# Local attention and an ELU feed-forward layer: the values of two neighbouring tiles in one visit, the global keys' values as 32-row products

## The chip, the cores and the metric

The kernel runs on one core of one Trainium2 chip. A core has five engines that run their own instruction streams: PE (TensorE, matrix products), DVE (VectorE), ACT (ScalarE), POOL (GpSimd) and SP (SyncE, which here issues the transfers). The metric is the device time of one execution in microseconds. Before the change it is 972.03 us, the median of three runs (970.75 to 972.27).

## The reference

Eight batches, eight heads of 64 dimensions, 512 local and 32 global positions, all float32. A global query looks at all 544 keys. A local query looks at the 32 global keys and at the local keys no more than 32 positions away. The attention's output is the input of two dense layers with an ELU between them.

```python
s_g = scale * q_g @ concat(k_g, k_l).T ;  out_g = softmax(s_g) @ concat(v_g, v_l)
s_ll = where(|i - j| <= 32, scale * q_l @ k_l.T, -1e9)
s_l = concat(scale * q_l @ k_g.T, s_ll) ;  out_l = softmax(s_l) @ concat(v_g, v_l)
x = concat(out_g, out_l) as (4608 tokens, 512)
h = x @ w_in                          # 512 -> 2048
g = where(h > 0, h, exp(min(h, 0)) - 1)
out = g @ w_out                       # 2048 -> 512
```

## The kernel before

**Two streams, woven together.** `attention()` and `ffn_stream()` are Python generators that emit instructions. The loop at L867 takes one step of attention, then as many steps of the feed-forward stream (FFN) as a table `PACE` asks for by then: none in the first 66 steps (the lead, flag `lead`), 180 by step 112, 850 by step 320. Small follow-up work (normalizing, reductions, splits into two float16 parts, conversion of the weights) is put off with `defer(n, fn)`: it is emitted n ticks later, and there is a tick at each FFN step, or at each attention step where no FFN step is due. A planner then orders each engine's queue by this order and its own estimate of when operands are ready, so that in the trace instructions can pass each other. Once attention has ended (flag `alone`), the rest of the FFN runs by itself.

**FFN.** A block is 256 tokens; there are 16 blocks of local tokens and one of all global tokens. `ffn1` (L315) multiplies float16 high and low parts of x and w_in, three products in place of one; the result goes through ACT and DVE (L324 to L357) and is split again. `ffn2` multiplies with w_out, either plainly (L390) or with seven half-size products in place of eight (`ffn2_seven`, L432), the latter once all weights are converted. From then on the seven's sums hold four PSUM banks: both `acc`, one of the two `h`, one of the four `pa`.

**Attention.** A tile is 128 local queries of four heads (one batch b, group of heads g, tile t of four). `slots` lists the tiles in order, with a slot "g" ahead for the global queries' scores of a batch and group (`stage_ga`, L641 and L644). In each slot the generator makes four steps, in the order "SVTU":

- **S**, `stage_s`, for the slot's own tile: scores for 64 own and 64 neighbouring keys and 32 global ones (L707), mask, scaling and minimum (L718 on DVE, into the buffer `p`, of which there are three), exponentials (L724 on ACT, deferred by 2 and 3), division by the sum (L731 on POOL and L733 on DVE, deferred by 4).
- **V**, `stage_v`, for the tile three slots back: the values.
- **T**, `stage_t`, for the tile two slots back: four transposes of the probabilities on PE (L747), copied from PSUM to `ptw` (L749). There are two `ptw` buffers.
- **U**, `stage_u`, for the same tile: transposes of the probabilities for global keys (L680) and of the global queries' probabilities (L683, L682), copied to `ptw` and to `ptg` (L684 to L691). `ptg` has one buffer for t = 0 and one for the other t; its last 32 columns, the global queries against global keys, are filled for t = 0 and stay zero in the other buffer.

**The value visit.** For each of the four heads h = 2j + r there are three products, all 128 rows deep and 64 columns wide, on column half r of the array. The first takes the global keys: `v[:, 8 + h, :]` holds the head's 32 global values in rows 32h to 32h + 31 and zeros elsewhere, and 160 columns of `ptg` hold all four heads' probabilities. The other two take the local keys, 96 columns each. All of a tile's products share one bank (`pv`; one of the `h` banks in the lead, a `pa` bank later). ACT copies the local queries' part to `xr` (L779); a tick later DVE adds the global queries' part to `xglob` (L784 for t = 0, L786 after) and takes the tile's absolute maximum (L788). After tile 1 or 3 of the second group a block of x is ready for the FFN; the global block's maximum is taken per two batches (L793).

**Loads.** SP issues every load and nearly every store in program order. `loads(i + 2)` fetches q, k and the global queries two slots ahead; v of a tile (L629, three buffers) is asked for in the tile's own slot, three slots ahead of its use. A transfer that waits for its buffer holds what stands behind it on SP.

Of the kernel before, what the change touches and what calls it, by code (L numbers as in the profile page):

```python
# [14 lines left out]
ALU = mybir.AluOpType  # L15
# [18 lines left out]
LAGT, LAGV = 2, 3  # L34
# [24 lines left out]
def attn_ffn(ctx: ExitStack, tc: tile.TileContext, qT, qgT, kT, vT, w_in, w_out, mask, out):  # L59
# [46 lines left out]
    ptw = [wts.tile([P, 2, 4 * (HQ + 32) + 32], F32, name=f"ptw{i}") for i in range(2)]  # L106
    ptg = [wts.tile([P, PW], F32, name=f"ptg{i}") for i in range(2)]
# [4 lines left out]
    for p in (*ptg, *pkd):  # L112
        nc.gpsimd.memset(p, 0.0)
# [185 lines left out]
    def ffn_stream():  # L299
# [203 lines left out]
        def split_x(blk):  # L503
            xr, mx = ready[blk]
            xh = ffn.tile([P, NC, BLK], F16, name="xh", bufs=NX)
            xl = ffn.tile([P, NC, BLK], F16, name="xl", bufs=NX)
            done = []
            xf, hf, lf = (a.rearrange("p c t -> p (c t)") for a in (xr, xh, xl))

            def s1():  # L510
                all_max(mx[:, 1:2], mx[:, 0:1])

            def s2():
                power(mx[:, 2:3], mx[:, 1:2])
# [7 lines left out]
            nc.vector.tensor_reduce(out=mx[:, 0:1], in_=mx[:, 6:10], op=ALU.max, axis=AX.X)  # L522
# [80 lines left out]
    def new_x():  # L603
        return ffn.tile([P, NC, BLK], F32, name="xr", bufs=3), ffn.tile([P, 10], F32, name="xm", bufs=NX + 4)

    xglob, mglob = wts.tile([P, NC, BLK], F32, name="xglob"), wts.tile([P, 10], F32, name="mglob")

    def attention():
# [17 lines left out]

        def load_v(b, g, t):
            v = apool.tile([P, 12, D], F32, name="v", bufs=3)
            nc.sync.dma_start(v, vT[b, g, t])  # L629
            return v  # L630
# [63 lines left out]
        def stage_s(st, g, t):  # L694
# [17 lines left out]
            pp = apool.tile([P, 4, KW], F32, name="p", bufs=LAGT + 1)  # L712
# [27 lines left out]
        def stage_t(st, g, t):  # L740

            n = tiles[0]
            tiles[0] += 1
            pt, pz = st["pt", g, t] = ptw[n % 2], ptg[t == 0]
            tp = ps_a.tile([P, 512], F32, name="pa")
            for h in range(4):
                nc.tensor.transpose(tp[:, h * P:(h + 1) * P], st["p", g, t][:, h, 0:P], ident)  # L747
# [4 lines left out]
        def stage_v(st, g, t):  # L752

            half = t // 2
            blk = 2 * st["b"] + half
            if (g, t % 2) == (0, 0):
                st["x", half] = new_x()
            xr, mx = st["x", half]
            v = st["v", g, t]
            pt, pz = st["pt", g, t]  # L760
            if lead[0]:
                pv = ps_h.tile([P, 2, BLK], F32, name="h").rearrange("p a b -> p (a b)")
            else:
                pv = ps_a.tile([P, 512], F32, name="pa")
            for j in range(2):
                for i in range(3):
                    for r in range(2):
                        h = 2 * j + r
                        at = j * PW
                        if i == 0:  # L770
                            w, x, o = v[:, 8 + h, :], pz[:, 0:GW], slice(at, at + GW)
                        elif i == 1:
                            w, x, o = v[:, h, :], pt[:, 0, 32 + 96 * h:128 + 96 * h], slice(at, at + 96)
                        else:
                            w, x, o = v[:, 4 + h, :], pt[:, 1, 96 * h:96 + 96 * h], slice(at + HQ, at + GW)
                        nc.tensor.matmul(pv[64 * r:64 * r + 64, o], w, x, start=i == 0, stop=i == 2)  # L776
            pv = pv[:, 0:2 * PW].rearrange("p (j a x) -> p j a x", j=2, a=2)
            xt = xr[:, 2 * g:2 * g + 2, t % 2 * P:(t % 2 + 1) * P]
            nc.scalar.copy(xt.rearrange("p j (a x) -> p j a x", a=2), pv[:, :, :, 0:HQ])  # L779
            xg = xglob[:, 2 * g:2 * g + 2, st["b"] * SG:(st["b"] + 1) * SG]  # L780

            def out():
                if t == 0:
                    nc.vector.tensor_copy(xg, pv[:, :, 0, HQ:])  # L784
                else:
                    nc.vector.tensor_add(xg, xg, pv[:, :, 0, HQ:])  # L786
                i = 6 + 2 * g + t % 2
                nc.vector.tensor_reduce(out=mx[:, i:i + 1], in_=xt, op=ALU.max, axis=AX.XY, apply_absolute_value=True)  # L788
                if g == 1 and t == NT - 1:
                    i = 6 + st["b"] // 2  # L790
                    if st["b"] % 2:
                        c = slice((st["b"] - 1) * SG, (st["b"] + 1) * SG)
                        nc.vector.tensor_reduce(out=mglob[:, i:i + 1], in_=xglob[:, :, c], op=ALU.max, axis=AX.XY,  # L793
                                                apply_absolute_value=True)
                if g == 1 and t % 2 == 1:
                    ready[blk] = xr, mx
                    if blk == NBL - 1:
                        ready[NBL] = xglob, mglob
# [13 lines left out]
        def loads(i):  # L812
# [3 lines left out]
            if s[0] == "g":  # L816
                st["qg", s[2]] = load_qg(s[1], s[2])
                for hp in (2 * s[2], 2 * s[2] + 1):
# [7 lines left out]

        for i in range(AHEAD):
            loads(i)
        for i in range(n + LAGV):
            if i + AHEAD < n:  # L830
                loads(i + AHEAD)
            s0 = slots[i] if i < n else None
            s1 = slots[i - LAGT] if LAGT <= i < n + LAGT else None
            s2 = slots[i - LAGV] if i >= LAGV else None
            for what in "SVTU":
                if what in "TU" and s1 and s1[0] == "l":
                    (stage_t if what == "T" else stage_u)(sts[s1[1]], *s1[2:])
                elif what == "V":
                    if s2 and s2[0] == "l":
                        stage_v(sts[s2[1]], *s2[2:])  # L840
                    if s0 and s0[0] == "l":
                        sts[s0[1]]["v", s0[2], s0[3]] = load_v(*s0[1:])
# [48 lines left out]
def _layout(q_l, k_l, v_l, q_g, k_g, v_g, moe_w_in, moe_w_out):  # L891
# [8 lines left out]
    vG = np.zeros((B, H, NT, 4, 32, D), f)  # L900
# [3 lines left out]
    for t in range(NT):  # L904
        for h in range(H):
            vG[:, h, t, h % 4] = v_g[:, h]
        for half in range(2):
# [3 lines left out]
            for c, key in enumerate([*own, *left, *right] if half == 0 else [*left, *right, *own]):  # L911
                if 0 <= key < SL:
# [7 lines left out]
    vT = np.concatenate([vW.reshape(B, 2, 4, NT, 2, P, D).transpose(0, 1, 3, 5, 4, 2, 6).reshape(B, 2, NT, P, 8, D),  # L920
                         vG.reshape(B, 2, 4, NT, P, D).transpose(0, 1, 3, 4, 2, 5)], axis=4)
    return dict(qT=qT, qgT=qgT, kT=kT, vT=vT, w_in=moe_w_in.view(np.int64), w_out=moe_w_out.view(np.int64), mask=mask)
# [17 lines left out]
```

## Time and profile before

| What | us |
|---|---|
| median of the runs shown (three) | 972.03 |
| the profiled execution | 972.96 |
| its span, first to last instruction | 970.9 |
| PE busy (matrix products) | 927.9, 96% of the span |
| DVE busy | 743.6, 77% |
| ACT busy | 691.7, 71% |
| POOL busy | 264.8, 27% |
| first FFN product (L315) starts at | 80.7 |
| last value product (L776) starts at | 832.9 |

The sum of a change is made against the profiled execution's 972.96 us. Busy times of PE overlap where products run side by side or are pipelined, so what a group of products costs is read from when instructions start, not from the sum of their durations. A row of a group gives the line, engine, operation, written and read tiles, shapes and count, then busy us and mean ns, then idle time just before and who ended it. In the shape of a product, 128*64 says how many rows and columns of the array it takes.

### The profile page before, as it was taken

The numbers are of one execution on the slowest core, as the hardware profiler recorded it, in microseconds if no ns is written. First come the engines' busy times: TensorE is split into PE (matmuls) and PEld (weight loads), VectorE is DVE, ScalarE is ACT, GpSimd is POOL, SyncE is SP. The second block draws the span as 40 slices with busy tenths as digits, with TensorE's granted clock in tenths as the row PEclk, the third lists the DMA queues.
The fourth block names the chain that finished last, engine by engine and source line by source line (L and its number), as shares of the span: only waits on it lengthen the run. The fifth ranks groups of instructions, "written<-read, shape, count | busy, mean of one in ns | idle before, by whom it ended". The sixth has DMA issues, their size and how long they took to land.

```text
span 970.9 us, 23721 instructions
## 1 busy us (share of the span) xinstructions
PE 927.9 (96%) x9216; PEld 742.1 (76%) x9216; DVE 743.6 (77%) x2147; ACT 691.7 (71%) x1666; POOL 264.8 (27%) x484
## 2 busy tenths in 40 slices
PE   5789889899999999999999999999999999999997
PEld 2557465566676788888888888888888888888886
DVE  4987899899957877677777877686777877676665
ACT  4777797776666777677777777677867767666674
POOL 3666193482222311231213122122222211200000
PEclk8889899999999999999999999999999999999999
DMA  6955766531342123111420133113311111000000
GB/s 246 326 189 169 250 235 222 180 122 70 117 146 86 56 94 128 42 32 48 152 98 19 56 108 134 34 41 110 110 57 32 42 34 39 2 22 23 2 23 22
DMA packets 39368, 95.09 MB, mean 98 GB/s; under 512 B 5944, under 2 KB 6456, under 8 KB 39256
## 3 DMA queue, kind: packets, MB, share of 16 engines
q1 hardware_dynamic: 39064, 93.32, 28.5%
q8 instruction: 72, 1.18, 0.5%
q14 instruction: 40, 0.33, 0.1%
q10 hardware_dynamic: 144, 0.13, 0.0%
q0 software_dynamic: 48, 0.13, 0.0%
HBM read 78.36 MB, written 15.20 MB: 96 GB/s over the span
## 4 chain that ended last, share of the span: by engine, by line
PE 72%; DVE 13%; issue 5%; ACT 5%; DMA 3%; POOL 2%; POOLq 0%; SPq 0%; DVEq 0%; ACTq 0%
PE h L315 26%; PE acc L432 13%; PE pa L776 7%; PE h L432 6%; PE acc L390 4%; PE pa L707 4%; PE pa L432 3%; PE pa L315 2%; PE pa L747 2%; DVE gl L336 2%; DMA raw<-w_in 1%; DVE cu L268 1%; PE h L776 1%; POOL p L731 1%; ACT p L724 1%
## 5 line engine op out<-in xcount | busy, mean ns | idle before, releaser
L315 PE MATMUL h<-xh,winh 128*128 128x256 f16 x992 | 270.6, 273 | 1.2 <-ACT hs L325 1.1
L315 PE MATMUL h<-xh,winl 128*128 128x256 f16 x992 | 270.4, 273 | 0.0
L315 PE MATMUL h<-xl,winh 128*128 128x256 f16 x992 | 270.4, 273 | 0.0
L315 PEld LDWEIGHTS <-winh 128*128 128x128 f16 x2176 | 208.1, 98 | 40.2 <-issue 9.5
L731 POOL TENSOR_SCALAR p<-p,sm 128x128 f32<-128x128 f32 x256 | 130.4, 526 | 370.2 <-DVE sm L729 212.7
L333 DVE SCALAR_TENSOR_TENSOR g<-g,hs 128x512 f32<-128x512 f32 x136 | 94.7, 696 | 113.7 <-ACT g L326 113.3
L432 PEld LDWEIGHTS <-gh 128*128 128x128 f16 x1456 | 139.2, 98 | 23.6 <-issue 6.1
L724 ACT ACTIVATE p<-p,m 128x160 f32<-128x160 f32 x256 | 106.5, 419 | 30.8 <-DVE m L718 30.2
L324 ACT ACTIVATE g<-h,xs 128x512 f32<-128x512 f32 x124 | 84.8, 684 | 57.7 <-PE h L315 57.4
L315 PEld LDWEIGHTS <-winl 128*128 128x128 f16 x1088 | 106.5, 98 | 12.9 <-issue 0.5
L336 DVE SCALAR_TENSOR_TENSOR gl<-gs,xs,gh 128x640 f16<-128x640 f32 x104 | 92.4, 888 | 26.8 <-ACT gh L355 26.5
L355 ACT ACTIVATE gh<-gs,xs 128x640 f16<-128x640 f32 x104 | 86.4, 831 | 36.1 <-DVE gs L351 36.0
L354 ACT ACTIVATE gh<-g,xs 128x256 f16<-128x256 f32 x104 | 53.2, 511 | 59.5 <-DVE g L333 57.7
L432 PE MATMUL acc<-wouth,gh 128*128 128x256 f16 (+1 forms) x312 | 88.0, 282 | 0.2 <-ACT gh L355 0.2
L326 ACT ACTIVATE g<-g 128x512 f32<-128x512 f32 x136 | 85.6, 630 | 0.0
L432 PE MATMUL acc<-wouth,gl 128*128 128x256 f16 x312 | 85.1, 273 | 0.2 <-DVE gl L336 0.2
L432 PE MATMUL acc<-woutl,gh 128*128 128x256 f16 x312 | 85.0, 273 | 0.0
L325 ACT ACTIVATE hs<-h,xs 128x512 f32<-128x512 f32 x124 | 84.5, 681 | 0.0
L336 DVE SCALAR_TENSOR_TENSOR gl<-g,xs,gh 128x256 f16<-128x256 f32 (+1 forms) x136 | 76.4, 562 | 7.0 <-ACT gh L340 6.2
L432 PEld LDWEIGHTS <-gl 128*128 128x128 f16 x728 | 71.2, 98 | 12.8 <-DVE gl L336 0.5
L718 DVE CUSTOM_DVE_ANT_0 p<-pa,msk 128x160 f32<-128x160 f32 x228 | 61.4, 318 | 3.3 <-PE pa L707 2.8
L390 PE MATMUL acc<-wouth,gh 128*128 128x512 f16 x128 | 49.8, 389 | 10.8 <-DVE o L398 6.3
(215 smaller groups left out, 2004.2 us busy)
## 6 DMA issues: line engine op xcount, KB each, us to landing
v<-vT SPq DMA_DIRECT2D x64, 384.0 KB, 3.2
k<-kT SPq DMA_DIRECT2D x32, 640.0 KB, 5.1
q<-qT SPq DMA_DIRECT2D x32, 256.0 KB, 5.7
raw<-w_in SPq DMA_DIRECT2D x8, 1024.0 KB, 5.8
raw<-w_out SPq DMA_DIRECT2D x8, 1024.0 KB, 5.7
out<-o SPq DMA_DIRECT2D x32, 256.0 KB, 2.3
od<-o SPq DMA_DIRECT2D x24, 256.0 KB, 2.3
o<-od SPq DMA_DIRECT2D x24, 256.0 KB, 2.7
```

Source lines behind the costliest of these rows:

```text
L315: nc.tensor.matmul(h[:, j, :], wt[:, c, f], xt[:, c, :], start=k == 0, stop=k == 11)
L324: nc.scalar.activation(g, hf, AF.Relu, scale=sc[:, p:p + 1])
L325: nc.scalar.activation(hs, hf, AF.Copy, scale=sc[:, 2 * NP + 1 + p:2 * NP + 2 + p])
L326: nc.scalar.activation(g, g, AF.Exp, scale=-1.0)
L333: nc.vector.scalar_tensor_tensor(out=g, in0=g, scalar=-1.0, in1=hs, op0=ALU.add, op1=ALU.max)
L336: nc.vector.scalar_tensor_tensor(out=dst, in0=src, scalar=sg, in1=hi, op0=ALU.mult, op1=ALU.subtract)
L355: nc.scalar.activation(gh[:, 2:7, :], s, AF.Copy, scale=sg)
L390: nc.tensor.matmul(acc[t], gt[:, s], wt[:, f, :], start=p == first and j == 0 and k == 0, stop=p == last and j == 1 and k == 2)
L432: nc.tensor.matmul(cols, gt, w, start=first, stop=last and k == len(todo) - 1)
L724: nc.scalar.activation(ps[i], ps[i], AF.Exp, bias=m[:, i:i + 1], scale=-1.0, accum_out=s[:, 0, i:i + 1])
L731: nc.gpsimd.tensor_scalar(ps[i][:, 0:P], ps[i][:, 0:P], s[:, 1, i:i + 1], 1.0, ALU.mult, ALU.mult)
L776: nc.tensor.matmul(pv[64 * r:64 * r + 64, o], w, x, start=i == 0, stop=i == 2)
```

## The change

The values of tiles 2*half and 2*half + 1 are computed in one visit, one slot behind the second tile's transposes. In each slot the order is now "TSUV". A pair uses two banks, one for each j (heads 0 and 1, heads 2 and 3), each with both tiles side by side. The global keys' products go first, one per head and tile: 32 rows deep (the head's rows of `ptg`, against the head's rows of a new tile `vg`), 64 columns wide, over 128 columns, or 160 where t = 0. The local keys' products follow as before. `v` loses its four global parts (384 KB to 256 KB a load) and is loaded in the slot of the tile's transposes; `vg` is loaded once per batch and group. ACT still makes two copies a pair, one per bank. DVE sums the global queries' parts of the two tiles with a reduction per bank, and takes one maximum over both tiles; the two halves of a batch are added once per batch. `ptw` and `ptg` get three buffers each, in turn; `ptg` needs no zeros. `p` goes from three buffers to two.

```diff
-LAGT, LAGV = 2, 3
+LAGT = 2
+NPT = 3
-    ptw = [... for i in range(2)]
-    ptg = [... for i in range(2)]
+    ptw = [... for i in range(NPT)]
+    ptg = [... for i in range(NPT)]
-    for p in (*ptg, *pkd):
+    for p in pkd:
         nc.gpsimd.memset(p, 0.0)
...
-            nc.vector.tensor_reduce(out=mx[:, 0:1], in_=mx[:, 6:10], op=ALU.max, axis=AX.X)
+            nc.vector.tensor_max(mx[:, 0:1], mx[:, 6:7], mx[:, 7:8])
...
+        def load_vg(b, g):
+            vg = apool.tile([P, D], F32, name="vg", bufs=3)
+            nc.sync.dma_start(vg, vgT[b, g])
+            return vg
         def load_v(b, g, t):
-            v = apool.tile([P, 12, D], F32, name="v", bufs=3)
+            v = apool.tile([P, 8, D], F32, name="v", bufs=3)
...
-            pp = apool.tile([P, 4, KW], F32, name="p", bufs=LAGT + 1)
+            pp = apool.tile([P, 4, KW], F32, name="p", bufs=LAGT)
...
-            pt, pz = st["pt", g, t] = ptw[n % 2], ptg[t == 0]
+            pt, pz = st["pt", g, t] = ptw[n % NPT], ptg[n % NPT]
...
+        def stage_v(st, g, half):
+            blk = 2 * st["b"] + half
+            if g == 0:
+                st["x", half] = new_x()
+                st["xg", half] = (apool.tile([P, NC, SG], F32, name="xg", bufs=1) if half
+                                  else xglob[:, :, st["b"] * SG:(st["b"] + 1) * SG])
+            xr, mx = st["x", half]
+            ts = (2 * half, 2 * half + 1)
...
+            vg = st["vg", g]
+            for s, t in ((1, ts[1]), (0, ts[0])):
+                pz = st["pt", g, t][1]
+                for h in (2, 3, 0, 1):
+                    j, r = divmod(h, 2)
+                    rows = slice(32 * h, 32 * h + 32)
+                    o, x = pv[j][64 * r:64 * r + 64, s * PW:(s + 1) * PW], pz[rows, :]
+                    if t == 0:
+                        o, x = o[:, 0:GW], x[:, 0:GW]
+                    else:
+                        o, x = (y.rearrange("p (a x) -> p a x", a=2)[:, :, 0:HQ] for y in (o, x))
+                    nc.tensor.matmul(o, vg[rows, :], x, start=s == 1, stop=False, skip_group_check=True)
+            for s, t in ((1, ts[1]), (0, ts[0])):
+                v, pt = st["v", g, t], st["pt", g, t][0]
+                for j in (1, 0):
+                    for i in range(2):
+                        for r in range(2):
+                            h = 2 * j + r
+                            at = s * PW + HQ * i
+                            x = pt[:, 0, 32 + 96 * h:128 + 96 * h] if i == 0 else pt[:, 1, 96 * h:96 + 96 * h]
+                            nc.tensor.matmul(pv[j][64 * r:64 * r + 64, at:at + 96], v[:, 4 * i + h, :], x,
+                                             start=False, stop=(s, i) == (0, 1), skip_group_check=True)
+            pv = [a[:, 0:2 * PW].rearrange("p (s a x) -> p s a x", s=2, a=2) for a in pv]
+            for j in range(2):
+                xt = xr[:, 2 * g + j, :]
+                nc.scalar.copy(xt.rearrange("p (s a x) -> p s a x", s=2, a=2), pv[j][:, :, :, 0:HQ])
+            xg = st["xg", half]
+            def out():
+                for j in range(2):
+                    nc.vector.tensor_reduce(out=xg[:, 2 * g + j, :], in_=pv[j][:, :, 0, HQ:].rearrange("p s x -> p x s"),
+                                            op=ALU.add, axis=AX.X)
+                nc.vector.tensor_reduce(out=mx[:, 6 + g:7 + g], in_=xr[:, 2 * g:2 * g + 2, :], op=ALU.max, axis=AX.XY,
+                                        apply_absolute_value=True)
+                if g == 1:
+                    ready[blk] = xr, mx
+                if g == 1 and half == 1:
+                    nc.vector.tensor_add(st["xg", 0], st["xg", 0], xg)
...
+        def load_values(i):
+            if 0 <= i < n and slots[i][0] == "l":
+                _, b, g, t = slots[i]
+                sts[b]["v", g, t] = load_v(b, g, t)
+        pairs = []
-        for i in range(n + LAGV):
+        for i in range(n + LAGT + 1):
             if i + AHEAD < n:
                 loads(i + AHEAD)
+            load_values(i - LAGT)
...
-            for what in "SVTU":
+            for what in "TSUV":
...
+                    if pairs:
+                        b, g, half = pairs.pop()
+                        stage_v(sts[b], g, half)
+                    if s1 and s1[0] == "l" and s1[3] % 2 == 1:
+                        pairs.append((s1[1], s1[2], s1[3] // 2))
```

More of the change, by code (lines that the diff above doesn't have):

```diff
@@ L58, in attn_ffn @@
 @with_exitstack
[L59 removed]
+def attn_ffn(ctx: ExitStack, tc: tile.TileContext, qT, qgT, kT, vT, vgT, w_in, w_out, mask, out):
     nc = tc.nc
@@ L761, in stage_v @@
             if lead[0]:
-                pv = ps_h.tile([P, 2, BLK], F32, name="h").rearrange("p a b -> p (a b)")
+                pv = [ps_h.tile([P, 2, BLK], F32, name="h").rearrange("p a b -> p (a b)") for _ in range(2)]
             else:
-                pv = ps_a.tile([P, 512], F32, name="pa")
-            for j in range(2):
[L766 to L780, printed above, removed]
-            def out():
[L783 to L792, printed above, removed]
+                pv = [ps_a.tile([P, 512], F32, name="pa") for _ in range(2)]
```

33 lines of the change are left out of this document (11 added, 22 removed).

## The prediction

> **What bounds the kernel now.** I read the busy time by stretches first, then PE's own waits, then PE's instructions in order of time around one value visit (L776). The stretches (length; busy us and instructions of PE, PEld, DVE, ACT, POOL; granted clock; DMA share; GB/s):
> ```profile
> 25.00:50.00 25.00, 19.37 (x217) 14.00 (x217) 23.56 (x85) 18.25 (x59) 16.88 (x27) 0.84 0.87 308
> 100.00:150.00 50.00, 43.06 (x358) 28.79 (x357) 45.94 (x114) 41.81 (x93) 31.18 (x40) 0.93 0.74 250
> 200.00:300.00 100.00, 97.17 (x823) 66.02 (x821) 85.14 (x189) 66.11 (x157) 33.48 (x50) 1.00 0.33 113
> 300.00:400.00 100.00, 100.00 (x1026) 79.42 (x1024) 75.73 (x230) 71.34 (x185) 23.48 (x46) 1.00 0.27 88
> 700.00:800.00 100.00, 100.00 (x1082) 84.69 (x1081) 76.86 (x237) 72.84 (x185) 25.16 (x50) 1.00 0.15 47
> ```
> Two regimes follow. Early, DVE is the fullest engine (23.56 of 25, 45.94 of 50) and PE has holes. From about 260 us PE is busy without a hole, while DVE and ACT have a quarter of their time free. A busy PE is not yet a PE at its peak, so I looked at whom PE waited for between 250 and 500 us:
> ```profile
> PE pa L129 <- DVE xm L522: 0.6, 1, 0.6
> PE acc L390 <- DVE o L398: 0.6, 1, 0.6
> PE h L315 <- ACT hs L325: 0.4, 1, 0.4
> ```
> That is 1.6 us in 250. PE's instruction stream sets the pace there, so a shorter stream is a shorter kernel. How many value visits lie in each regime (L776 alone: length, PE, PEld, clock, DMA):
> ```profile
> 80.00:260.00 180.00, 15.43 (x240) 13.31 (x240) 0.97 0.53 177
> 260.00:835.00 575.00, 62.67 (x1056) 54.39 (x1056) 1.00 0.22 73
> ```
> A float32 product is two matmul records, a tile has 12 products, so 24 records: 44 tiles (22 pairs) lie where PE is the bound, 10 tiles (5 pairs) in the mixed stretch, and the other 10 of the 64 before 80 us.
>
> **The value visits, now and after.** One visit, with the FFN product before and after it (start, duration, instruction):
> ```profile
> 301.74 0.38 PE L390 MATMUL acc<-wouth,gl 128*128 128x512 f16 x1
> 302.05 0.49 PE L776 MATMUL pa<-ptg,v 128*64 128x160 f32 x4
> 302.38 0.50 PE L776 MATMUL pa<-ptw,v 128*64 128x96 f32 x8
> 302.70 0.44 PE L776 MATMUL pa<-ptg,v 128*64 128x160 f32 x4
> 302.98 0.50 PE L776 MATMUL pa<-ptw,v 128*64 128x96 f32 x8
> 303.41 0.28 PE L315 MATMUL h<-xh,winh 128*128 128x256 f16 x1
> ```
> Durations overlap, so the starts count. A 512-column float16 product streams for about 0.22, so PE could have gone on at 301.96; it began at 302.05 (0.09 to enter the 128x64 tiling). The eight 96-column records took 302.70 - 302.38 = 0.32: two at a time (heads r = 0 and 1 have different columns of the array), 0.08 each, 0.83 ns a column. By that rate the 160-column records need 2 x 0.133 = 0.27 for four. Streaming is 2 x (0.27 + 0.32) = 1.18; the whole is 303.41 - 301.96 = 1.45; so 0.27 is entering and leaving, 0.09 + 0.18. **A pair costs 2.90 now.**
>
> The change moves the global keys' products to 32-row tiles: four heads, each on its own 32 rows, on two column halves, into two banks. No row shows 32x64. The nearest are the 64x32 scores of the global queries and the 64x64 local scores:
> ```profile
> 310.03 0.66 PE L641 MATMUL pa<-k,qg 64*32 64x256 f32 x8
> 310.49 0.25 PE L644 MATMUL pa<-k,qg 64*32 64x32 f32 x7
> 310.55 0.38 PE L641 MATMUL pa<-k,qg 64*32 64x256 f32 x1
> ...
> 320.56 0.78 PE L707 MATMUL pa<-k,q 64*64 64x160 f32 x16
> 321.26 0.39 PE L390 MATMUL acc<-wouth,gh 128*128 128x512 f16 x1
> ```
> The first half of L641 and L644 takes 310.55 - 310.03 = 0.52: eight records of 256 columns at 0.213, eight of 32 at 0.027. One by one that is 1.92, four at a time 0.48. L707: sixteen of 160 columns at 0.133 are 2.13 one by one, 0.53 four at a time, and 0.70 was taken, the 0.18 of leaving included. Both run four abreast, and L707's two row groups share column halves and differ in bank, as heads 2 and 0 will.
>
> So I take four abreast. Odd tiles and the later even ones stream 128 columns (the empty 32 are left out): 8 records at 0.107, four abreast, 0.21 a tile; the first tile of a row of tiles keeps 160 columns, 0.27, and lies in every second pair. Mean of a pair: 0.45. The value products don't change: 32 records of 0.08, two abreast, 1.28. Between the two tilings there is one more switch. A visit's two switches cost 0.09 and 0.18; this one gets 0.18, bounds 0.09 and 0.27. **A pair after: 0.09 + 0.45 + 0.18 + 1.28 + 0.18 = 2.18; gain 0.72**, of which 0.27 is the second entry and exit, 0.63 the shorter global part, less 0.18. Times 22: **15.8 us**. Bounds: switch at 0.09, 0.81 x 22 = 17.8. Two abreast only: 0.45 more, 0.27 x 22 = 5.9. One by one: 1.36 more, a loss of 0.64 x 22 = 14.
>
> The Trainium skill, TensorEngine Tiling (Array Packing), Restrictions and Gotchas, has a rule against the four abreast: different row tiles cannot access the same PSUM bank at the same time. Heads 2 and 3 share a bank here, 0 and 1 another, so by it the sum would be the 5.9. The trace disagrees: L641's two row groups write one bank (other partitions) and took 0.52 where taking turns would need 0.96. I keep four abreast, and give the rule a chance because it speaks of 32-row tiles too.
>
> **DVE and ACT.**
> ```profile
> L788 DVE TENSOR_REDUCE xm<-xr 128x1 f32<-128x256 f32 x64 | 26.0, 407 | 0.0
> ...
> L779 ACT COPY xr<-pa 128x256 f32<-128x256 f32 x54 | 19.4, 360 | 4.6 <-PE pa L776 4.6
> ...
> L195 DVE TENSOR_REDUCE cm<-cu 128x1 f32<-128x1024 f32 x8 | 9.6, 1205 | 0.0
> ...
> L786 DVE TENSOR_TENSOR xglob<-xglob,pa 128x64 f32<-128x64 f32 x41 | 8.6, 211 | 0.9 <-ACT xr L779 0.9
> ...
> L691 DVE TENSOR_REDUCE ptg<-pa 128x32 f32<-128x128 f32 x16 | 4.5, 281 | 0.0
> ```
> A pair on DVE now: 2 x (211 + 407) = 1236 ns. After: one maximum over 512, 407 + 256 x (1205 - 407)/768 = 673, and two sums of 64 into 32 from PSUM, 281 - 64 x 1.04 = 214 each: 1101. A batch saves 4 x 135 less one addition of 128 elements (some 300): 0.24 us. Behind PE (DVE a quarter free) this is nothing; in the 20 tiles before 260 us, 2.5 batches, 0.6 us. ACT keeps two 360-ns copies a pair, now back to back. Removing the two ptg memsets and adding a third ptw's falls in POOL's start-up, ahead of its first use; the one-element maximum replaces a one-element reduce: nothing. In the mixed stretch PE's 5 x 0.72 = 3.6 counts only where PE sets the pace; I take 1.2, bounds 0 and 3.6.
>
> **Loads and order.** A tile's v load moves from three slots ahead of its use to one or two, loses a third of its bytes, and 16 loads of vg join (32 KB, like qg).
> ```profile
> SPq L629 <- PE pa L776: 308.0, 46, 20.0
> ```
> ```profile
> v<-vT SPq DMA_DIRECT2D x64, 384.0 KB, 3.2
> ```
> SP's 308 us of waiting are a v load held until the value visit before frees its buffer, with k, q, weights and outputs queued behind it. After, two buffers hold a pair and the third is free for the next even tile; the odd tile's load follows the visit that frees its buffer by a slot. So that wait shrinks. From load to use are at least 7 of the generator's steps, four to a slot; at 575 / 44 = 13.1 us a tile that covers 3.2 several times. Without this cover a late v would hold PE. Values become ready two steps later per block; FFN has other blocks in hand.
>
> The step that I trust least is the lead. T of a tile now comes ahead of S two tiles later, 7 steps after its own S (was 10), and p has two buffers, not three: DVE can't write tile k+2's scores until PE has transposed tile k. PE in the lead:
> ```profile
> 8.14 0.50 PE L707 MATMUL acc<-k,q 64*64 64x160 f32 x8
> ...
> 40.32 1.35 PE L707 MATMUL pa<-k,q 64*64 64x160 f32 x16
> ...
> 42.33 1.14 PE L707 MATMUL acc<-k,q 64*64 64x160 f32 x16
> ...
> 50.71 0.47 PE L747 MATMUL pa<-ident,p 128*128 128x128 f32 x1 [0.76 <-POOL p L731]
> ...
> 57.18 0.66 PE L747 MATMUL pa<-ident,p 128*128 128x128 f32 x4
> ...
> 80.69 0.27 PE L315 MATMUL h<-xh,winh 128*128 128x256 f16 x1
> ```
> The lead's 13 tiles take 80.69 - 8.14 = 72.6 us, 5.6 each. The sixth tile's scores start at 40.32 and its last transpose, which waited for POOL's scaling, ends at 51.18: 10.9 us for the loop. Two buffers then allow a tile per 5.45 us, just under the 5.6 of now. The seventh took 42.33 to 57.84, 15.5, partly since it wasn't urgent. Loop at 10.9: nothing; at 15.5: 13 x (7.75 - 5.6) = 28 lost. The earlier and smaller loads, worth at most about 3, stand against it. I take +2, nearest to the loop that really waited; bounds -3 and +28.
>
> **Sum.** 15.8 + 0.6 + 1.2 - 2 = 15.6. The profiled execution took 972.96 (span 970.9): 957.4. The median of the runs shown is 0.9 lower: **956.5 us**.
>
> **Rivals.**
> 1. Two abreast, as the page's rule has it. The first row group waits for the second to leave the bank. For it: no 32-row row exists. Against it: L641. Gain 5.9 + 0.6 + 0.5 - 2 = 5: 967.
> 2. The lead becomes bound by p's two buffers. Place: DVE's L718 behind PE's L747 behind POOL's L731. With a loop of 13.4, 13 x 1.1 = 14 lost: about 968. From a loop of 2 x (5.6 + 17.6/13) = 13.9 us the whole gain is gone; at 15.5 the kernel takes 972 - 17.6 + 28 = **982, slower**. For it: DVE 94% busy between 25 and 50 us, so a late small instruction waits behind conversions. Against it: 10.9 when it was urgent.
> 3. A new wait in PE's stretch. A pair holds two of the four pa banks until ACT's two copies and DVE's three reductions end; the FFN's evacuation on ACT queues behind 0.36 more. At 0.36 in every pair: 8 us back, 964.
> 4. The 32-row products one by one: 14 lost there, 986. Both rows of narrow tilings speak against it.
>
> **How the numbers follow.** The forecast has 0.60, rival 1 0.10, rival 2 0.14 (half of it slower or level), rival 3 0.12, rival 4 0.04. The forecast's own range is 949 (switch at 0.09, all of 3.6 counted, loads helping) to 961. Rival 3 and rivals 1 and 2's milder half end by 968; above lie rival 4 and the harder half of 2, 0.11, and below 949 little. Range 949 to 968. Three runs lie within 1.5 us, so 0.2% (2 us) is about what can be told from no change. Slower 0.10, same 0.05, faster 0.85.
>
> **What would show it.** After 300 us, a value visit as one block of 16 records of 32x64 and 32 of 128x64, from entry to the next FFN product about 2.2 us, half as often; the 32-row block near 0.45 (0.9 says rival 1, 1.8 rival 4). PE without waits from 260 us on, or else L315 or L707 waiting for ACT's or DVE's reads of the pv banks (rival 3). The first L315 between 78 and 85 us; near 100 with PE or DVE idle until POOL p L731 says rival 2. I am wrong altogether if the block is short and the end doesn't come earlier by that much: then PE's stream did not set the pace.

## The result and the profile after

The changed kernel takes **980.67 us**, the median of four runs (979.69 to 981.74), against 971.42 for the kernel before on the same chips: a ratio of 1.0092 [1.0078, 1.0105]. It is slower by 0.9%, where 956.5 us was forecast. The profiled execution took 979.8 us, with a span of 978.0; it lies 6.8 us above the profiled execution before, where the medians are 9.2 apart. One of the ten executions of run 9 below took 3195.66 us: the median of that run has it in, its ratio leaves it out.

To see where the time went I cut both spans at two events that exist in each kernel: the first FFN product (end of the lead) and the first of the seven products that reads the added-up weights (`acc<-cu`), where the plain second layer gives way to the seven-product form. The three stages are called lead, middle and late. For every run below they are those of its one profiled execution.

| Kernel | Lead | Middle | Late | Span |
|---|---|---|---|---|
| before | 80.7 | 253.2 | 637.0 | 970.9 |
| after | 90.7 | 251.1 | 636.2 | 978.0 |
| after less before | +10.0 | -2.1 | -0.8 | +7.1 |

The two cuts in the timeline of PE after (start, duration, instruction), and the second of them before:

```profile
90.68 0.27 PE L316 MATMUL h<-xh,winh 128*128 128x256 f16 x1
...
341.81 0.38 PE L433 MATMUL acc<-cu,gh 128*128 128x256 f16 x2
```
```profile
333.87 0.38 PE L432 MATMUL acc<-cu,gh 128*128 128x256 f16 x2
```

So there are two questions: what lengthened the lead by 10 us, and why the long late stage, in which most pairs lie, gained 0.8 us. The busy time by stretches, with the columns of the prediction's first fence:

```profile
25.00:50.00 25.00, 18.69 (x199) 10.75 (x199) 23.62 (x82) 17.12 (x55) 11.37 (x19) 0.77 0.76 278
100.00:150.00 50.00, 42.27 (x393) 28.23 (x391) 44.51 (x126) 43.26 (x104) 28.26 (x43) 1.00 0.70 232
...
300.00:400.00 100.00, 99.64 (x1015) 77.59 (x1013) 76.95 (x225) 71.62 (x183) 24.00 (x45) 1.00 0.25 84
700.00:800.00 100.00, 97.47 (x1061) 81.90 (x1059) 75.26 (x232) 72.28 (x180) 24.17 (x46) 1.00 0.14 47
```

PE issues fewer matmul records between 700 and 800 us (1061 for 1082). A pair has as many of them as two visits had (16 + 32 for 2 x 24), so the stream did not get shorter there but slower, and 97.47 of 100 where it was 100.00 says that PE now waits.

**The value visit itself is as forecast.** PE around one pair:

```profile
315.16 0.38 PE L391 MATMUL acc<-wouth,gl 128*128 128x512 f16 x1
315.47 0.67 PE L782 MATMUL pa<-ptg,vg 32*64 32x128 f32 x16
316.06 1.54 PE L791 MATMUL pa<-ptw,v 128*64 128x96 f32 x32
317.54 0.39 PE L391 MATMUL acc<-wouth,gh 128*128 128x512 f16 x1
```

From 315.47 to 317.54 are 2.07 us, and 0.09 to enter as before, so 2.16 (2.18 forecast, 2.90 before). The sixteen 32-row records with the switch behind them take 316.06 - 315.47 = 0.59. Four abreast they need 16 x 0.107 / 4 = 0.43, which leaves 0.16, put down to the switch; two abreast they alone would need 0.85.

**Whom PE waits for.** In the lead, after (0 to 91 us) and before (0 to 81 us); each row gives total us, times, longest:

```profile
PE pa L753 <- POOL p L737: 20.8, 10, 4.3
```
```profile
PE pa L747 <- POOL p L731: 4.8, 3, 3.7
```

In the late stage (345 to 845 us), after and before:

```profile
PE h L316 <- ACT hs L326: 6.6, 10, 1.0
PE pa L782 <- ACT pg L664: 1.3, 2, 0.8
PE pa L686 <- DVE ptw L755: 0.6, 2, 0.4
```
```profile
PE h L315 <- ACT hs L325: 0.7, 2, 0.4
```

**The lead.** PE's attention work ahead of the first FFN product is the same in both kernels: the scores of 13 tiles, 44 transposes, the values of 10 tiles. The transposes L753 wait 16.0 us longer for POOL's division of `p`. Some other waits of the kernel before are gone, so PE's waits grow by some 7 us in all (20.2 to 27.0); the rest of the 10 is a start later by 0.5 and products that run longer, at a granted clock of 0.75 in place of 0.79 (mean between 8 us and the end of the lead). One such place, PE and then POOL:

```profile
37.37 0.48 PE L713 MATMUL acc<-k,q 64*64 64x160 f32 x2
37.89 0.68 PE L753 MATMUL pa<-ident,p 128*128 128x128 f32 x2
39.54 0.68 PE L753 MATMUL pa<-ident,p 128*128 128x128 f32 x2 [0.98 <-POOL p L737]
40.05 0.27 PE L130 MATMUL pa<-ident,wm_a 128*128 128x128 f32 x1
40.26 0.77 PE L713 MATMUL acc<-k,q 64*64 64x160 f32 x14
```
```profile
36.55 3.28 POOL L737 TENSOR_SCALAR p<-p,sm 128x128 f32<-128x128 f32 x4 [3.18 <-ACT cu L179]
```

The fourteen score records at 40.26 don't read `p`; two of their tile had run at 37.37 (a product is two records). They stand behind the transposes in PE's stream, which runs in order, so the late division delays the next tile's scores, and with them its exponentials and its own division. (The row's ACT cu is not what the division reads: the reciprocals of the sums, which it does read, ended on DVE at 36.36.)

**The late stage.** Adding up PE's timeline from each start to the next:

| PE in the late stage, us | before | after |
|---|---|---|
| values (39 tiles; 40 tiles after) | 52.9 | 44.9 |
| FFN products, waits and the entry into a narrow tiling included | 516.2 | 521.0 |
| scores (one tile more after, 0.7) | 25.8 | 28.0 |
| all else | 42.1 | 42.4 |

Twenty pairs without waits would have cost 41.8, and 19 fewer entries into the narrow tilings save 1.7: 12.8 us were there to gain. The visits took 3.1 of it for waits inside them (44.9 for 41.8), the FFN 6.5 (521.0, where 516.2 less 1.7 was to come), the scores 2.2, of which 0.7 is the tile more.

Nearly all of the FFN's loss is the wait for `h`, 6.6 us where it was 0.7. One case on ACT, and on PE; the last product into that `h` bank (L316) started at 655.94 and took 0.27:

```profile
657.24 0.51 ACT L355 ACTIVATE gh<-g,xs 128x256 f16<-128x256 f32 x1
657.64 0.82 ACT L356 ACTIVATE gh<-gs,xs 128x640 f16<-128x640 f32 x1
658.37 0.68 ACT L325 ACTIVATE g<-h,xs 128x512 f32<-128x512 f32 x1
658.93 0.68 ACT L326 ACTIVATE hs<-h,xs 128x512 f32<-128x512 f32 x1
```
```profile
655.94 0.27 PE L316 MATMUL h<-xh,winl 128*128 128x256 f16 x1
...
658.56 0.27 PE L433 MATMUL pa<-raw,gl 128*128 128x256 f16 x1
659.67 0.27 PE L316 MATMUL h<-xh,winh 128*128 128x256 f16 x1 [0.84 <-ACT hs L326]
```

In the seven-product form one `h` bank is left for the first layer. It is full at 656.21; ACT comes to read it at 658.37, 2.16 us late, and has it free at 659.61. PE had 21 of the second layer's products as cover (656.05 to 658.67), and no attention step happened to stand there. Taken over all blocks of that stage, ACT picks `h` up 0.29 us late on average before the change (8 times of 76 over 1 us) and 0.75 us after (22 times of 77).

### The profile page after: what moved, and what is told of

The parts are those of the page before. It is cut to its first block, busy times and chain, and to the rows that moved or that the text cites. A ratio compares the mean times of both kernels' runs of the same rounds, so it can differ in the third digit from the quotient of the medians.

```text
span 978.0 us, 23682 instructions
## 1 busy us (share of the span) xinstructions
PE 918.7 (94%) x9216; PEld 726.0 (74%) x9216; DVE 746.5 (76%) x2120; ACT 690.0 (71%) x1667; POOL 272.6 (28%) x484
## 3 DMA queue, kind: packets, MB, share of 16 engines
q1 hardware_dynamic: 41368, 85.46, 25.8%
## 4 chain that ended last, share of the span: by engine, by line
PE 56%; ACT 16%; DVE 14%; issue 6%; DMA 4%; POOL 3%; SPq 0%; POOLq 0%; ACTq 0%; DVEq 0%
PE h L316 22%; PE acc L433 9%; PE h L433 5%; PE pa L791 3%; PE pa L713 3%; PE acc L391 3%; PE pa L316 2%; PE pa L433 2%; PE pa L753 2%; ACT p L730 2%; ACT g L325 2%; DMA raw<-w_in 2%; DVE g L334 2%; ACT hs L326 2%; POOL p L737 2%
## 5 line engine op out<-in xcount | busy, mean ns | idle before, releaser
L316 PE MATMUL h<-xh,winh 128*128 128x256 f16 x992 | 271.6, 274 | 7.7 <-ACT hs L326 6.7
L316 PE MATMUL h<-xl,winh 128*128 128x256 f16 x992 | 271.3, 274 | 0.0
L316 PE MATMUL h<-xh,winl 128*128 128x256 f16 x992 | 271.3, 274 | 0.0
L316 PEld LDWEIGHTS <-winh 128*128 128x128 f16 x2176 | 210.9, 98 | 47.4 <-issue 16.5
L737 POOL TENSOR_SCALAR p<-p,sm 128x128 f32<-128x128 f32 x256 | 133.2, 536 | 348.0 <-DVE sm L735 185.6
L316 PEld LDWEIGHTS <-winl 128*128 128x128 f16 x1088 | 106.9, 98 | 13.4 <-issue 0.5
L355 ACT ACTIVATE gh<-g,xs 128x256 f16<-128x256 f32 x104 | 52.9, 509 | 65.8 <-DVE g L334 64.6
L753 PE MATMUL pa<-ident,p 128*128 128x128 f32 x256 | 48.5, 296 | 25.7 <-POOL p L737 25.2
L724 DVE CUSTOM_DVE_ANT_0 p<-pa,msk 128x160 f32<-128x160 f32 x228 | 61.6, 317 | 9.9 <-PE pa L713 9.9
```

The costliest lines, as they stand in the source:

```text
L316: nc.tensor.matmul(h[:, j, :], wt[:, c, f], xt[:, c, :], start=k == 0, stop=k == 11)
L724: nc.vector.tensor_tensor_reduce(out=p, in0=sp[r][:, j * KW:(j + 1) * KW], in1=msk[:, mi, :], op0=ALU.add, op1=ALU.min, scale=-scale, scal ...
L737: nc.gpsimd.tensor_scalar(ps[i][:, 0:P], ps[i][:, 0:P], s[:, 1, i:i + 1], 1.0, ALU.mult, ALU.mult)
```

## The experiments

All times below are medians, ratios are against the kernel before on the same chip, with a 95% interval. All of these kernels compute the whole reference. The first four ask which part of the change lengthened the lead, and whether the late waits come from the order, from the pair or from where the exponentials fall.

**1. The kernel before with the new order and two buffers of `p`, values still tile by tile.**

```diff
-            pp = apool.tile([P, 4, KW], F32, name="p", bufs=LAGT + 1)
+            pp = apool.tile([P, 4, KW], F32, name="p", bufs=LAGT)
-            for what in "SVTU":
+            for what in "TSVU":
```


> The kernel before, with only two things of the change: the steps of a slot in the order T, S, V, U, and two buffers for p in place of three. Values stay one tile a visit. Theory A (the lead is lengthened because T stands ahead of S and p has two buffers): the first FFN product moves from 80.7 to about 91 us and the time goes from 971 to about 981. Theory B (the lead is lengthened by the pair visits, which hold both h banks, or by the later v loads): the first FFN product stays at 80 to 82 us and the time within 2 us of 971.

989.55 us, 1.0176 [1.0141, 1.0210]. Stages 88.9, 262.4, 636.5. The lead is 8.2 longer with no pair in it, so it takes no pair to lengthen it. The time is 8.5 above the 981 that theory A gave, since the middle is 9.2 longer too. In the late stage PE waits for nothing, so the order alone does not make the wait for `h`.

**2. After, with three buffers of `p`** (and two of `v`, whose third has no room beside it).

```diff
-            v = apool.tile([P, 8, D], F32, name="v", bufs=3)
+            v = apool.tile([P, 8, D], F32, name="v", bufs=2)
-            pp = apool.tile([P, 4, KW], F32, name="p", bufs=LAGT)
+            pp = apool.tile([P, 4, KW], F32, name="p", bufs=LAGT + 1)
```


> The changed kernel with three buffers for p again; since the buffers don't fit beside the rest, v gets two in place of three. Theory A1 (of the two, the buffers are the cause): the first FFN product comes back from 90.7 to 81 to 83 us and the time from 980.7 to about 971. Theory A2 (the order is the cause: PE stands at a transpose that isn't ready while scores behind it are): it stays at 88 to 92 and the time within 3 us of 980. A v load that waits for the pair visit could cost up to 2 us by itself.

983.15 us, 1.0108 [1.0067, 1.0148]; stages 93.8, 252.3, 636.3. The third buffer gives nothing back; the lead's granted clock was 0.70 in this execution. As `v` lost one, this alone does not clear the two buffers of `p`; runs 5 and 6 look at them by themselves, in the kernel before.

**3. After, with S ahead of T again.**

```diff
-            for what in "TSUV":
+            for what in "STUV":
```


> The changed kernel with the steps of a slot in the order S, T, U, V; p keeps two buffers. Theory A2 (order): first FFN product back at 81 to 83 us, time about 971. Theory A1 (buffers): DVE still can't write the scores before the transposes two tiles back, first FFN product at 88 to 92, time within 3 us of 980.

974.04 us, 1.0028 [1.0002, 1.0054]; stages 83.7, 255.3, 633.3. With two buffers of `p` and the pairs kept, 7.0 of the lead's 10.0 us come back by putting the scores ahead of the transposes. The middle loses 4.2.

**4. After, with the exponentials and divisions one tick later outside the lead.**

```diff
-                defer(2 + i // 2, ...)
+                defer(2 + i // 2 + (not lead[0]), ...)
-            defer(4, norm)
+            defer(4 + (not lead[0]), norm)
```


> The changed kernel with the exponentials and the normalization of a tile put off by one tick more, outside the lead only. After 340 us PE waits 6.7 us for ACT's evacuation of h, in 10 places, and in the three that were read the exponentials stand ahead of it on ACT, twice waiting for DVE. Theory C (this place in ACT's queue is the cause): the wait of L316 for ACT falls below 2 us, the time to about 976; the first FFN product stays at 90 to 91. Theory D (ACT is late since the pair visit took away PE work that covered the evacuation, whatever stands ahead): the wait stays at 5 to 8 us and the time within 2 us of 980.

990.16 us, 1.0172 [1.0127, 1.0217]; stages 91.2, 261.1, 636.5. PE still waits 6.7 us in 10 for `h` in the late stage: the theory that the exponentials' place makes this wait has fallen. The middle became 10.0 longer, which neither theory had. PE's waits there grew from 16.5 to 21.3 us, of which the wait for the division is 1.1 (4.4 to 5.5), and the granted clock was 0.95 where it had been 0.98; what makes the rest is not shown.

**5 and 6. The kernel before with the order alone, and with the two buffers alone.**

```diff
-            for what in "SVTU":
+            for what in "TSVU":
```


> The kernel before with the order T, S, V, U alone; p keeps three buffers, values one tile a visit. With order and two buffers together the first FFN product stood at 88.9 us (80.7 before) and the time was 17 us longer. If the order is the cause by itself: first FFN product at 86 to 92 us, time 983 to 990. If it needs both: 80 to 84 us, 970 to 976.


```diff
-            pp = apool.tile([P, 4, KW], F32, name="p", bufs=LAGT + 1)
+            pp = apool.tile([P, 4, KW], F32, name="p", bufs=LAGT)
```


> The kernel before with two buffers for p alone, the order as it was. If the buffers are the cause by themselves: first FFN product at 86 to 92 us, time 983 to 990. If the order is: 80 to 84 us and 970 to 976.

The order alone (two executions): 988.05 us, 1.0178 [1.0156, 1.0200]; stages 83.6, 265.7, 636.6. The buffers alone (three executions): 975.44, 1.0041 [1.0021, 1.0060]; stages 82.2, 253.2, 638.6. PE's wait for the division up to the second cut, order alone and then buffers alone:

```profile
PE pa L747 <- POOL p L731: 30.9, 19, 7.8
```
```profile
PE pa L747 <- POOL p L731: 4.5, 2, 4.1
```

The wait is 4.8 in the kernel before. It comes with the order, not with the buffers, and the order alone costs as much as both together (1.0178 and 1.0176). Where it costs came out differently: with three buffers 2.9 us in the lead and 12.5 in the middle, with two 8.2 and 9.2. The wait does not explain that: in the lead it is 20.9 us with three buffers and 19.0 with two. Run 5 had the time of one theory and the lead of the other. The buffers alone have a lead 1.5 longer, which is less than one execution can tell (see run 10).

**7 and 8. After, with V earlier.** If the late stage turns on which steps stand next to the pair, other orders must move it, though each step's work is the same.

```diff
-            for what in "TSUV":
+            for what in "STVU":
```


> The changed kernel with the order S, T, V, U. S stands ahead of T as before the change, and each step that takes two of the three free pa banks (S, V) has a step with one bank between it and the next. If the order is what costs the lead, the first FFN product comes at 81 to 85 us. If the waits in the late stage are for banks that the step just ahead still holds, the value visits keep their 2.1 us, S loses the 3.7 us that it waited with the order S, T, U, V, and the late stage takes 624 to 629 us (before 637, with S, T, U, V 633): time 962 to 968. If the late stage's gain is lost for another reason, it stays at 632 to 637 and the time at 972 to 976.


```diff
-            for what in "TSUV":
+            for what in "SVTU":
```


> The changed kernel with the order S, V, T, U, the order of the kernel before. The lead as with S, T, V, U: 81 to 85 us. S and V, two banks each, now stand next to each other with three free banks. By the theory of the banks V waits for S's scores to be read, 0.5 us or more in each of 20 visits of the late stage, which takes 632 us or more, and the time is 970 or more. If neighbours don't matter, the late stage is as short as with S, T, V, U.

S, T, V, U: 973.51 us, 1.0032 [1.0016, 1.0047]; stages 89.2, 250.6, **629.8**. S, V, T, U: 982.27, 1.0108 [1.0078, 1.0138]; stages 83.7, 255.9, **643.2**. The late stage moves by 13.4 us by order alone. The 962 to 968 us expected of S, T, V, U did not come, as its lead stayed at 89.2. Whom PE waits for in the late stage, first S, T, V, U, then S, V, T, U:

```profile
PE pa L782 <- ACT pg L664: 2.1, 3, 1.0
PE h L316 <- ACT hs L326: 0.8, 3, 0.4
```
```profile
PE pa L782 <- DVE m L724: 3.5, 5, 1.1
PE pa L782 <- ACT pg L664: 2.3, 4, 0.8
PE h L316 <- ACT hs L326: 1.5, 4, 0.6
PE pa L782 <- DVE xglob L801: 1.2, 3, 0.5
```

With V right behind S, a visit asks for two `pa` banks while DVE is still reading scores (L724), or ACT those of the global queries (L664), out of the others; the seven's sums hold the fourth. PE then does half a visit and returns for the other half:

```profile
500.57 0.65 PE L782 MATMUL pa<-ptg,vg 32*64 32x128 f32 x8
501.16 0.88 PE L791 MATMUL pa<-ptw,v 128*64 128x96 f32 x16
501.97 0.28 PE L316 MATMUL h<-xh,winh 128*128 128x256 f16 x1
...
503.65 0.65 PE L782 MATMUL pa<-ptg,vg 32*64 32x128 f32 x8 [0.64 <-ACT pg L664]
504.24 0.88 PE L791 MATMUL pa<-ptw,v 128*64 128x96 f32 x16
```

A pair split so enters and leaves the narrow tilings twice: PE made 29 visits for the 20 pairs of the stage, and the values took 54.5 us, 7.0 of them waits (44.9 after, 43.7 with S, T, V, U, both in 20 visits). S, T, V, U keeps the pair whole and also brings the wait for `h` from 6.6 down to 0.8: the late stage is 7.2 shorter than before the change.

**9 to 11. One order in the lead, another behind it.**

```diff
-            for what in "TSUV":
+            for what in ("SVTU" if lead[0] else "TSUV"):
```


> The changed kernel with S, V, T, U in the lead and its own order T, S, U, V after it. If T ahead of S costs in the lead alone: first FFN product at 83 to 85 us, middle stage about 251, late stage about 636 as in the changed kernel, time about 974. If it costs as much in the middle stage (there the kernel before lost 12 us to the order alone), the first FFN product comes at 84 but the middle stage takes 255 to 263 and the time is 978 to 985.


```diff
-            for what in "TSUV":
+            for what in ("SVTU" if lead[0] else "STVU"):
```


> The changed kernel with the order S, V, T, U in the lead (there the value visits take the h banks, so S and V don't share banks) and S, T, V, U after it. If the lead's length follows from the order in the lead alone, the first FFN product comes at 83 to 85 us as with S, V, T, U throughout; if the late stage follows from the order after the lead alone, it takes 629 to 631 us as with S, T, V, U throughout. Both: time 964 to 968, 3 to 6 us under the kernel before. If each order only shifts the planner's choices by chance, the lead stands at 88 or more or the late stage at 633 or more, and the time is 970 to 976.


```diff
-            for what in "TSUV":
+            for what in ("STUV" if lead[0] else "STVU"):
```


> The same with S, T, U, V in the lead and S, T, V, U after it. The same two theories: first FFN product at 83 to 85 us and late stage 629 to 631, time 964 to 968; or lead or late stage off by 3 us and more, time 970 to 976.

| Order in the lead, then | Lead | Middle | Late | us | Ratio |
|---|---|---|---|---|---|
| S V T U, T S U V | 81.2 | 250.3 | 636.2 | 971.77 | 1.0012 [0.9992, 1.0033] |
| S V T U, S T V U | 86.0 | 252.4 | 630.0 | 965.94 | 0.9953 [0.9938, 0.9967] |
| S T U V, S T V U | 84.8 | 254.7 | 629.9 | 972.56 | 1.0017 [0.9993, 1.0042] |

The first row changes nothing but the order in the lead of the changed kernel and takes 8.9 us off the median: the lead's loss is the order there. Its first FFN product:

```profile
81.24 0.27 PE L316 MATMUL h<-xh,winh 128*128 128x256 f16 x1
```

How the order lengthens the lead is shown only in part. The lead after, that of run 9 and that of run 10:

```profile
8.00:90.70 82.70, 57.35 (x607) 36.16 (x604) 60.47 (x241) 52.15 (x177) 42.32 (x86) 0.75 0.55 192
```
```profile
8.00:81.20 73.20, 51.40 (x603) 34.87 (x597) 59.35 (x241) 51.96 (x177) 44.02 (x88) 0.77 0.61 211
```
```profile
8.00:86.00 78.00, 56.37 (x607) 38.84 (x603) 59.55 (x242) 52.06 (x177) 42.77 (x88) 0.69 0.59 203
```

PE waits 27.0 us in the lead after and 24.1 in that of run 9, so the waits make only 2.9 of the 9.4 between them. The rest is that the same products run longer: PE is busy 57.35 us for 51.40. The granted clock in these leads is on record as 1.0 or 0.5 and nothing between; of its busy time PE had 29.5 us at 0.5 after, and 22.7 in run 9. It also differs at one order: run 10 has the order of run 9 in the lead and waits of 23.0, but 34.1 us at 0.5, and its lead is 4.8 longer. That execution took 970.12, 4.2 over the median of its kernel, so its 86.0 is not typical; and a few us between the leads of two single executions tell little, where the medians tell more.

The late stage keeps its 630 whatever stands in the lead. The third row missed its forecast of 964 to 968: its middle took 254.7 where the same order had 250.6 (run 7) and 252.4 (run 10), and why is not shown.

**12. After, with DVE in ACT's place for `hs` in the seven-product stage,** to see whether the wait for `h` is ACT being too full.

```diff
-            nc.scalar.activation(hs, hf, AF.Copy, scale=sc[...])
+            if seven is None or alone[0]:
+                nc.scalar.activation(hs, hf, AF.Copy, scale=sc[...])
+            else:
+                nc.vector.tensor_scalar(hs, hf, sc[...], 1.0, ALU.mult, ALU.mult)
```


> The changed kernel, but from the seven-product blocks to the end of attention DVE, not ACT, makes hs, the second of the two reads that free the h bank (L326), so that the two reads run side by side. In the changed kernel ACT took up a finished h bank 0.75 us late on the mean of 77 (0.29 of 76 in the kernel before), and PE waited 6.6 us for it in 10 places. If the 6.6 us are ACT's lateness at the h bank: the wait for h falls below 2 us and the late stage from 636 to 629 to 632 us, unless DVE, some 55 us fuller, comes late itself. If the wait only moves (to DVE's read of h, or to gh and gl), the late stage stays at 635 to 638.

989.02 us, 1.0188 [1.0168, 1.0208]; late stage 644.5. PE now waits for DVE:

```profile
PE h L316 <- DVE hs L329: 13.5, 12, 2.4
PE acc L436 <- DVE gl L340: 1.5, 2, 0.8
```

The wait moved with the instruction and doubled. This swap is no cure: DVE comes to `h` 1.55 us late on average, ACT, with less to do, 0.57.

**13. The best order of each stage.**

```diff
-            for what in "TSUV":
+            for what in ("SVTU" if lead[0] else "STVU" if "f" in tab else "TSUV"):
```


> The changed kernel with the order S, V, T, U in the lead, T, S, U, V between the lead and the seven-product blocks, and S, T, V, U from there on: for each stage the order that took least there. If the stages add up, the first FFN product comes at 81 us, the middle stage takes 250 and the late stage 630: time 963, 7 to 9 us under the kernel before, 3 under the kernel with two orders. If the planner's choices in one stage hang on what follows, the lead or the middle stage is 3 to 6 us longer and the time 966 to 970.

**964.61 us, 0.9941 [0.9923, 0.9960]**: faster than both kernels, with the pairs and everything else of the change kept. Stages 81.6, 251.6, 629.9; they are those of runs 9, after and 7 within 1 us, so these three add up (in run 11 the middle did not). Against the kernel before: +0.9, -1.6, -7.1. Two of its stretches:

```profile
300.00:400.00 100.00, 98.97 (x1048) 78.55 (x1041) 76.70 (x230) 72.57 (x188) 25.49 (x46) 1.00 0.24 82
700.00:800.00 100.00, 99.62 (x1096) 84.69 (x1095) 75.69 (x240) 74.28 (x191) 23.69 (x47) 1.00 0.10 34
```

PE issues 1096 records between 700 and 800 us, for 1082 before and 1061 after: what the pairs save has become a faster stream.

## Why the prediction was wrong, point by point

**Four abreast, and the price of a pair: right.** 2.16 us for 2.18, with a switch of 0.16 for the 0.18 taken. The forecast had named what would mean something else: a short block, and an end that doesn't come earlier. That is what came.

The Trainium skill, TensorEngine Tiling (Array Packing), Restrictions and Gotchas, has it that row tiles may not access one PSUM bank at the same time. By it the 32-row block would have needed 0.85 us (an estimate, 8 turns of 0.107) and the switch; the trace shows 0.59 with the switch, so the rule isn't seen here for heads 2 and 3 in one bank and 0 and 1 in another.

**DVE's terms: right.** Rows of the groups after:

```profile
L803 DVE TENSOR_REDUCE xm<-xr 128x1 f32<-128x512 f32 x32 | 21.6, 674 | 0.0
...
L801 DVE TENSOR_REDUCE xg<-pa 128x32 f32<-128x64 f32 x28 | 5.1, 214 | 1.2 <-ACT xr L796 1.1
...
L808 DVE TENSOR_TENSOR xglob<-xglob,xg 128x128 f32<-128x128 f32 x8 | 2.2, 279 | 0.0
```

674, 214 and 279 ns, for 673, 214 and 300. The v loads were no trouble either: SP's wait of 308.0 us for v buffers fell to 165.4, though 81.6 came for the buffers of `vg`, and PE never waits for a load of either.

**"The step that I trust least", the lead at +2: wrong.** It measured +10.0. Rival 2 had the place (PE's transposes behind POOL's division), but not the cause, and that the measured time lies near its 982 is luck: it set 28 us lost in the lead against a whole gain of 17.6, where 10.0 were lost and 2.9 gained. It looked for a loop through two buffers of `p`; those alone have a lead 1.5 us longer (run 6). The prediction named the other half itself, that T comes ahead of S and 7 steps after its own S where it was 10, and then priced only the loop. What it left out is the queue: while T waits, the next tile's scores stand behind it though they need nothing from it. With the order S, V, T, U there and the two buffers kept the lead is 81.2 (run 9), so the order is the cause. That the queue is the whole of the way is not shown: PE's wait for the division falls from 20.8 to 4.7 us by it, but PE's waits in all only from 27.0 to 24.1, and the rest went with a higher granted clock; in run 5 the wait is 20.9 and the lead 83.6. Whether the buffers add to the order is open as well: the kernel before has 83.6 with three and 88.9 with two, and run 2 had to give up a buffer of `v`.

**"PE's instruction stream sets the pace there, so a shorter stream is a shorter kernel", 15.8: wrong.** The late stage had 12.8 us of it to gain and gained 0.8, so PE's stream alone did not set the pace. The 1.6 us of waits in 250 were read as if all else had room. They hold as well where PE's own work is only just long enough to hide ACT's and DVE's readings of PSUM. A visit removed between two uses of the one free `h` bank is 1.4 us of that cover gone, and the pair puts two visits' work in one place; this is the reading, and the runs show its two ends, that the waits come with the pairs (none in run 1) and that they go with the order (run 7). **Rival 3** named the mechanism, two banks held by a pair and ACT's evacuation coming later, with 8 us back; given 0.12, it was the one that came in this stage: 6.5 in the FFN, 5.9 of it by `h`, 3.1 inside the visits, 1.5 at the scores. Its 8 us were about 11, and its path was only half right: it argued from 0.36 us more of ACT's copies, but run 12 shows the wait following the instruction to another engine, and runs 7, 8 and 13 show that the place of the steps decides.

**The middle, 0.6 + 1.2: right** in size, -2.1 for -1.8. But it is a sum of two that were not foreseen: the order costs the kernel before 9.2 there with the same two buffers (run 1), so the pair and what came with it gave back some 11 (251.1 against 262.4). That the two nearly cancel to the forecast is luck.

**What stays open.** Why PE waits 0.8 us for `h` with S, T, V, U and 6.6 with T, S, U, V is not settled. ACT's lateness doesn't tell: it is 0.61 us on average against 0.75, and over 1 us in 22 of 77 times with either order, so the difference would lie in PE's cover, which was not followed; the planner's reordering of each engine's queue lies between. The lead of S, T, V, U is not settled either: it is 89.2, where that of S, T, U, V and of S, V, T, U is 83.7, though S stands ahead of T in all three. PE's wait for the division is 10.0 us there (6.6 and 6.1) and the granted clock 0.73 (0.75 and 0.77); no run separates the two.

## What to carry to other kernels

An engine's queue runs in order, so a step that waits for a late operand holds up ready steps behind it: here the order S, V, T, U in place of T, S, U, V, in the lead alone, was worth 8.9 us. S ahead of T is not enough by itself, as S, T, V, U shows, so such an order is to be run and not only argued. An engine that never waits may still be covering another's latency; before its work is taken out, look at what must be read out of PSUM in that time and how many banks the neighbouring steps hold. After such a removal the order of the steps is to be tried again, stage by stage: it turned +0.9% into -0.6%.

## What the runs showed of the hardware that was not expected

Going from a 32x64 to a 128x64 tiling costs about 0.16 us within a visit (an estimate, 0.59 less 0.43), near to the 0.18 that leaving the narrow tilings costs before an FFN product. And four 32-row tiles, two of them in each of two banks, run together: sixteen records of 128 columns took 0.59 us with that switch. In the lead the granted clock stood at either 1.0 or 0.5, and the share of each differed between kernels with the same steps there: 22.7 us of PE's busy time at 0.5 in run 9, 34.1 in run 10, with a lead of 81.2 and 86.0.
